# Loading two time steps at once, and only the rows that hold data, in a linear-attention and mixture-of-experts kernel

## The chip, the cores and the metric

The kernel runs on one core of a Trainium2 chip. The metric is the device time of one execution in microseconds. A comparison of this kernel with another can tell about 0.2% from no change.

The engines are called PE (matrix multiply; PEld is its weight load), DVE (vector), ACT (scalar), POOL (general purpose) and SP (which here only issues DMAs). Each engine works through its own list of instructions in order, and waits at an instruction until the semaphores it needs are set.

## The reference

The input is `r`, `k`, `v` of shape (4 batches, 8 heads, 768 tokens, 48), a decay `w` and a bonus `u` for each head and channel. The first half is a recurrence over the tokens, with a 48x48 state for each batch and head:

```python
for t in range(S):
    kt, vt, rt = (k[:, :, t], v[:, :, t], r[:, :, t])
    cur = np.einsum('bhd,bhe->bhde', u[None] * kt, vt)
    y[:, :, t] = np.einsum('bhd,bhde->bhe', rt, state + cur)
    state = w[None, :, :, None] * state + np.einsum('bhd,bhe->bhde', kt, vt)
```

The second half takes the 3072 rows of `y` (384 wide). Rows with `x @ w_skip > 0` go to one of 8 experts by the largest of `x @ w_gate`, and become `x + gate * (relu(x @ w1[e]) @ w2[e])`; the others stay as they are.

## The kernel before

**Recurrence.** The tokens are cut into chunks of 64. Two batches go together, so there are 2 x 12 = 24 steps (`NT`), step n being chunk `n % 12` of pair `n // 12`. A step needs two inputs:

- `dm`: r and k of the chunk, channels on the partitions. Two heads share a tile: rows 0 to 47 hold the channels of one, rows 64 to 111 those of the other, and rows 48 to 63 and 112 to 127 are zeros, which lie in device memory too. A step is 128 rows of 4096 bytes, one DMA of 512 KB (`load_dm`, L277), into one of four rotating buffers.
- `v`: 64 tokens of each of two batches, the tokens on the partitions. It lies in a tile `vz` whose other quadrants are zeros, written once at the start by POOL (L323), so that one matrix multiply can treat both batches. A step is two DMAs of 64 rows, 96 KB each (`load_v`, L285), into one of four lasting tiles.

**Work of a step.** `prep_r` (DVE, L418) and `prep_k` (POOL, L436) scale r and k by powers of the decay into `rd` and `kd`. On PE, `scores` (L448) multiplies them, `across` (L534) applies the state, `turn_k` (L461) transposes `kd` for the state update, `state` (L481) and `within` (L510) multiply by `v`. ACT copies the result out of PSUM (`evac`, L545), and SP writes it to device memory with two DMAs (L563; steps 4 to 7 write a third, of 192 KB).

**Order.** The order is written by hand. Iteration n of the main loop first issues on SP `load_dm(n + 5)`, `load_v(n + 4)` and in 15 of the iterations a 256 KB piece of an expert's weights (`raw`, L110). Then come `scores(n + 1)`, `across(n + 1)`, on POOL the splitting of an earlier weight piece into a high and a low part, `turn_k(n + 2)`, `prep_k(n + 3)`, `prep_r(n + 3)`, `state(n + 1)`, `within(n + 1)` and `evac(n + 1)` with its output DMAs. So `dm` of step n + 5 is issued in iteration n, scaled in iteration n + 2, and its `kd` first read by PE in iteration n + 3; `v` of step n + 4 is issued in iteration n and read by `state(n + 4)` in iteration n + 3.

A DMA on SP takes one of eight completion semaphores in turn, so each DMA waits until the one eight places before it has landed.

**Experts.** After step 23 the routed rows are gathered and the eight experts follow, with weights loaded and split ahead. Their first scratch tiles take the places of the `dm` buffers (`scratch`, L848) and of `vz`.

Of the kernel before, what the change touches and what calls it, by code (L numbers as in the profile page):

```python
# [9 lines left out]
F32 = mybir.dt.float32  # L10
# [10 lines left out]
B, H, S, D = 4, 8, 768, 48  # L21
N, DM, E, F = B * S, H * D, 8, 1024
P = 128
C = 64
# [4 lines left out]
NHP = H // 2  # L29
NT = NPAIR * NSTEP  # L30
# [8 lines left out]
DR = P  # L39
ADV = NB * NHP  # L40
BIG = 4 * N
NVK = 4
GB = 4
BH = 2
NDM = 4
# [16 lines left out]
def tile_wkv_moe(  # L62
# [11 lines left out]
    nc = tc.nc  # L74
# [168 lines left out]
        mix(y, q)  # L243


    lctx = ExitStack()
    ld = lctx.enter_context(tc.tile_pool(name="ld", bufs=NDM, side="right"))
    vctx = ExitStack()
    vp = vctx.enter_context(tc.tile_pool(name="vp", bufs=1, side="right"))
    with ExitStack() as actx:  # L250
# [17 lines left out]
        ub_sb = tab.tile([DR, NHP], F32, name="ub_sb")  # L268
        nc.scalar.dma_start(out=ub_sb, in_=ub)

        loaded = {}
        vz = [vp.tile([P, 2, 2, NHP, D], F32, name=f"vz{j}") for j in range(NVK)]

        def load_dm(n):
            pr, i = divmod(n, NSTEP)
            d = ld.tile([P, 2, NHP, 2, C], F32, tag="dm", name=f"dm{n}", bufs=NDM)
            nc.sync.dma_start(out=d, in_=dm[pr, i])  # L277
            loaded[n] = [d[:DR], None]

        def load_v(n):  # L280
            pr, i = divmod(n, NSTEP)
            t = vz[n % NVK]
            for q in range(2):
                half = slice(q * C, (q + 1) * C)
                nc.sync.dma_start(out=t[half, q], in_=tok[pr, i, half])  # L285
            loaded[n][1] = t

        load_dm(0)
        load_dm(1)
        load_v(0)  # L290
        load_dm(2)
        load_v(1)
        load_dm(3)
        load_v(2)
        load_v(3)
        wgp = tab.tile([P, NCC, 2, C // 2], F32, name="wgp")
        pick = tab.tile([P, 2, NB, E + 1], F32, name="pick")

# [21 lines left out]
        eye = lower("eye", ALU.is_equal)  # L320
        for t in vz:
            for q in range(2):
                nc.gpsimd.memset(t[(1 - q) * C : (2 - q) * C, q], 0.0)  # L323

        w_d = tab.tile([DR, NSUB, 2, NHP, C], F32, name="w_d")

# [85 lines left out]
                nc.scalar.mul(rd[:, :, 1], rd[:, :, 0], uw[:, hp : hp + 1])  # L412

        def prep_r(n, parts=(0, 1)):
            d = loaded[n][0]
            if 0 in parts:
                rds[n] = wk.tile([DR, NHP, 2, 2, C], F32, tag="rd", name=f"rd{n}", bufs=4)
                nc.vector.tensor_tensor(  # L418
                    rds[n][:, :, :, 0],
                    d[:, 0],  # L420
                    w_d[:, n % NSUB, 0][:, :, None].to_broadcast([DR, NHP, 2, C]),
                    ALU.mult,
                )
            if 1 in parts:
                rd = rds[n]
                nc.vector.tensor_tensor(
                    rd[:, :BH, :, 1],
                    rd[:, :BH, :, 0],
                    (uw if n < 3 else uw_p)[:, :BH, None, None].to_broadcast([DR, BH, 2, C]),
                    ALU.mult,  # L430
                )

        def prep_k(n, eng=None):
            d = loaded[n][0]
            kds[n] = wk.tile([DR, NHP, 2, C], F32, tag="kd", name=f"kd{n}", bufs=4)
            (eng or nc.gpsimd).tensor_tensor(  # L436
                kds[n],
                d[:, 1],
                w_d[:, n % NSUB, 1][:, :, None].to_broadcast([DR, NHP, 2, C]),
                ALU.mult,  # L440
            )
# [28 lines left out]
            nc.vector.copy_predicated(shape(am[n % 2]), eye, p[:, :, 1])  # L470

        def state(n):
            t = loaded[n][1]
            i, sub = n % NSTEP, n % NSUB
            if i == NSTEP - 1:
                return
            kt = kts.pop(n)
            s, nxt = ps_s[:, : 2 * NHP * D].rearrange("p (q f) -> p q f", q=2), sblk[(n + 1) % 2]
            for hp in range(NHP):
                for a in range(2):  # L480
                    nc.tensor.matmul(  # L481
                        s[a * C : (a + 1) * C, :, hp * D : (hp + 1) * D],
                        kt[:, hp, a, :],
                        t[:, :, a, hp, :],
                        start=i == 0 and hp == 0,
                        stop=True,
                        skip_group_check=True,
                    )
            if sub < NSUB - 1:
                nc.scalar.copy(nxt, s)  # L490
                return
            heads = lambda t: t.rearrange("p q (h e) -> p q h e", h=NHP)
            nc.vector.tensor_tensor(
                heads(nxt), heads(s), wh_sb[:, None, :, None].to_broadcast([P, NB, NHP, D]), ALU.mult
            )
            return lambda: nc.scalar.copy(s, nxt)
# [5 lines left out]
        def place_y(a, c):  # L502
            return ps_y[c * C : (c + 1) * C, a, : NHP * D].rearrange("p (q g e) -> p q g e", q=NB, g=NHP // 2)

        def within(n, behind=None):
            t = loaded[n][1]
            for g in range(NHP // 2):
                for a, c in FOUR:
                    hp = 2 * g + (a ^ c)
                    ins = nc.tensor.matmul(  # L510
                        place_y(a, c)[:, :, g, :],
                        am[n % 2][:, a, hp * C : (hp + 1) * C],
                        t[:, :, a, hp, :],
                        start=g == 0 and n % NSTEP == 0,
                        stop=True,
                        skip_group_check=True,
                    )
                    if behind is not None:
                        tc.add_manual_dep(
                            ins.ins,  # L520
                            behind.name,
                            mybir.DependencyInfo(mybir.DependencyClass.Sync, mybir.DependencyReason.DATA),
                            reason="other row tiles write these banks",
                        )
                        behind = None
# [320 lines left out]
            return banks[kind][(used[kind] - 1) % len(banks[kind])]  # L846

        def scratch(name, shape, dt, tag):  # L848
            return (ld if tag == "dm" else scr[0]).tile(
                [P] + shape, dt, tag=tag, name=name, bufs=NDM if tag == "dm" else 3  # L850
            )

        scr = []
# [14 lines left out]
        def piece(j, split=False):  # L868
            e, j = divmod(j, NPC)
            if split:  # L870
                split_piece(e, j, nc.gpsimd)
            else:
                load_piece(e, j)
# [15 lines left out]
        mask_scores(0)  # L889
        load_dm(4)  # L890
        state(0)
        turn_k(1)
        warm(1)
        within(0)
        evac(0)
        load_v(4)
        nc.sync.dma_start(out=wgp, in_=wgq)
        prep_r(2)
        bonus(2, BH)
        prep_k(2)  # L900
        grow(3)
        for n in range(NT - 1):
            if n + 5 < NT:
                load_dm(n + 5)
            if n + 4 < NT and n:
                load_v(n + 4)
            if n in LOADS:
                piece(LOADS.index(n))
            scores(n + 1)
# [37 lines left out]
        done = NPC  # L947
        piece(len(LOADS))
        vctx.close()
        scr.append(lctx.enter_context(tc.tile_pool(name="scr", bufs=3, side="right", reuse_waits="tile")))  # L950
        first = begin(0, "dm")

# [378 lines left out]
```

## Time and profile before

| what | value |
|---|---|
| median of 3 runs | 266.89 us (266.56 to 266.95) |
| profiled execution, its own time | 264.4 us |
| span in that execution, first to last instruction | 262.6 us |
| PE busy | 247.9 us (94%) |
| POOL, DVE, ACT busy | 131.7, 181.0, 140.5 us |
| moved by DMA | 53.92 MB, 205 GB/s over the span |
| first `scores` of the loop; last | 12.06 us; 107.12 us |
| granted PE clock | 0.996 |

The profile is one execution. Busy times of different engines overlap. A share of busy time averages over a recurrence of some 110 us and an expert stage of some 150 us, so stretches have to be looked at one by one. In the rows below, "A <- B" says that A stood idle until B, and the number is that idle time. SPq rows are DMA issues: their time is what SP spends on issuing, not the transfer.

### The profile page before, as it was taken

The numbers are of one execution on the slowest core, as the hardware profiler recorded it, in microseconds if no ns is written. First come the engines' busy times: TensorE is split into PE (matmuls) and PEld (weight loads), VectorE is DVE, ScalarE is ACT, GpSimd is POOL, SyncE is SP. The second block draws the span as 40 slices with busy tenths as digits, with TensorE's granted clock in tenths as the row PEclk, the third lists the DMA queues.
The fourth block names the chain that finished last, engine by engine and source line by source line (L and its number), as shares of the span: only waits on it lengthen the run. The fifth ranks groups of instructions, "written<-read, shape, count | busy, mean of one in ns | idle before, by whom it ended". The sixth has DMA issues, their size and how long they took to land.

```text
span 262.6 us, 8820 instructions
## 1 busy us (share of the span) xinstructions
PE 247.9 (94%) x3594; PEld 228.5 (87%) x3594; DVE 181.0 (69%) x366; ACT 140.5 (53%) x314; POOL 131.7 (50%) x130
## 2 busy tenths in 40 slices
PE   7799999989999999998999999999999999999990
PEld 2698898977988989877899899999999999999980
DVE  7976667786888989674567997979277484692210
ACT  2555667757865767434658628358085381660200
POOL 8656424547555365405689818454535355345011
PEclk9999999999999999999999999999999999999998
DMA  6978779899987897767798896877648475001000
GB/s 195 268 225 253 216 223 272 264 255 269 273 256 226 257 245 243 204 189 243 222 308 261 267 325 206 261 238 244 215 143 255 141 228 199 20 1 47 1 34 21
DMA packets 31137, 53.92 MB, mean 205 GB/s; under 512 B 4603, under 2 KB 14471, under 8 KB 31088
## 3 DMA queue, kind: packets, MB, share of 16 engines
q1 hardware_dynamic: 28896, 48.09, 60.5%
q0 software_dynamic: 2048, 5.18, 6.5%
q8 instruction: 30, 0.49, 0.8%
q14 instruction: 19, 0.16, 0.2%
q10 hardware_dynamic: 144, 0.00, 0.0%
HBM read 45.46 MB, written 8.39 MB: 205 GB/s over the span
## 4 chain that ended last, share of the span: by engine, by line
PE 82%; DMA 5%; DVE 4%; ACT 2%; POOL 2%; issue 1%; SPq 0%; POOLq 0%; DVEq 0%; ACTq 0%
PE ps_y L170 11%; PE ps_p L170 10%; PE ps_p L448 7%; PE ps_y L510 6%; PE ps_s L481 6%; PE ps_p L160 5%; PE ps_r L160 5%; PE ps_l L160 5%; PE ps_y L160 5%; PE ps_l L461 4%; PE ps_y L534 3%; PE ps_t L577 3%; PE ps_l L605 2%; POOL kd L436 2%; DMA xg<-out_dram,gid 2%; DMA raw<-in_w_dram 2%
## 5 line engine op out<-in xcount | busy, mean ns | idle before, releaser
L116 POOL TENSOR_TENSOR lo<-raw,hi 128x512 fp32r<-128x512 f32 x40 | 52.8, 1324 | 39.8 <-ACT hi L115 39.6
L115 ACT CAST hi<-raw 128x512 fp32r<-128x512 f32 x96 | 54.7, 623 | 1.9 <-DMA raw<-in_w_dram 1.7
L116 DVE TENSOR_TENSOR lo<-raw,hi 128x512 fp32r<-128x512 f32 x56 | 51.1, 936 | 2.5 <-ACT hi L115 2.3
L436 POOL TENSOR_TENSOR kd<-dm,w_d 128x512 f32<-128x512 f32 x23 | 33.6, 1460 | 31.5 <-DMA dm<-in_dm_dram 14.5
L178 POOL DMA_INDIRECT out_dram<-xg,sid x16 | 17.4, 1084 | 37.6 <-DVE xg L175 29.1
L469 DVE COPY_PREDICATED am<-below,ps_p 128x512 f32<-128x512 int8 x24 | 17.7, 736 | 13.4 <-PE ps_p L448 13.2
L448 PE MATMUL ps_p<-rd,kd 64*64 64x128 f32 x768 | 26.7, 276 | 0.0
L128 POOL DMA_INDIRECT xg<-out_dram,gid x16 | 18.5, 1153 | 15.3 <-DMA raw<-in_w_dram 10.6
L164 ACT ACTIVATE hh<-ps_p 128x464 fp32r<-128x464 f32 x7 | 3.9, 559 | 37.7 <-PE ps_p L160 35.7
L418 DVE TENSOR_TENSOR rd<-dm,w_d 128x512 f32<-128x512 f32 x24 | 21.9, 912 | 3.1 <-DMA dm<-in_dm_dram 3.1
L448 PEld LDWEIGHTS ps_p<-rd,kd 64*64 64x64 f32 x768 | 20.9, 133 | 3.3 <-issue 1.2
L510 PE MATMUL ps_y<-vz,am 128*64 128x96 f32 x384 | 20.3, 248 | 0.9 <-DVE am L470 0.7
L463 ACT COPY kt<-ps_l 128x512 f32<-128x512 f32 x22 | 12.9, 585 | 14.2 <-PE ps_l L461 13.9
L412 ACT ACTIVATE rd<-rd,uw 128x128 f32<-128x128 f32 x50 | 17.2, 394 | 6.0 <-DVE rd L418 5.6
L170 PE MATMUL ps_p<-hi,hh 128*128 128x384 f32 x56 | 19.4, 347 | 0.0
L170 PE MATMUL ps_p<-hi,hl 128*128 128x384 f32 x56 | 19.0, 340 | 0.4 <-DVE hl L165 0.4
L481 PE MATMUL ps_s<-vz,kt 128*64 128x96 f32 x352 | 19.4, 253 | 0.0
L170 PE MATMUL ps_y<-hi,hh 128*104 128x384 f32 x56 | 18.9, 338 | 0.0
L510 PEld LDWEIGHTS ps_y<-vz,am 128*64 128x64 f32 x384 | 17.2, 137 | 1.9 <-DVE am L470 1.1
L170 PE MATMUL ps_y<-hi,hl 128*104 128x384 f32 x56 | 18.9, 337 | 0.0
L170 PE MATMUL ps_y<-lo,hh 128*104 128x384 f32 x56 | 18.9, 337 | 0.0
L170 PE MATMUL ps_p<-lo,hh 128*128 128x384 f32 x56 | 18.8, 336 | 0.0
(252 smaller groups left out, 653.1 us busy)
## 6 DMA issues: line engine op xcount, KB each, us to landing
raw<-in_w_dram SPq DMA_DIRECT2D x96, 256.0 KB, 4.0
dm<-in_dm_dram SPq DMA_DIRECT2D x24, 512.0 KB, 5.4
vz<-in_tok_dram SPq DMA_DIRECT2D x48, 96.0 KB, 4.8
out_dram<-xt SPq DMA_DIRECT2D x48, 96.0 KB, 4.1
out_dram<-xt SPq DMA_DIRECT2D x4, 192.0 KB, 4.3
xg<-out_dram,gid POOLq DMA_INDIRECT x16, 4.8
out_dram<-xg,sid POOLq DMA_INDIRECT x16, 3.7
wgp<-in_wgq_dram SPq DMA_DIRECT2D x1, 96.0 KB, 2.1
```

The lines of the kernel that those rows point to most:

```text
L115: nc.scalar.copy(hi, t)
L116: eng.tensor_tensor(lo, t, hi.bitcast(F32), ALU.subtract)
L128: ins = nc.gpsimd.indirect_dma_start(out=xg[:m], out_offset=None, in_=out[0:rows], in_offset=bass.IndirectOffsetOnAxis(ap=gid[:m, q : q + ...
L160: nc.tensor.matmul(ph, a[:, c, fs], b[:, c, :], start=(k == 0), stop=(k == 3 * NCC - 1))
L170: nc.tensor.matmul(py, a, b[:, f, :], start=(k == 0), stop=(k == 3 * NFC - 1))
L178: ins = nc.gpsimd.indirect_dma_start(out=out, out_offset=bass.IndirectOffsetOnAxis(ap=sid[: listed(q), q : q + 1], axis=0), in_=xs.pop(q)[ ...
L418: nc.vector.tensor_tensor(rds[n][:, :, :, 0], d[:, 0], w_d[:, n % NSUB, 0][:, :, None].to_broadcast([DR, NHP, 2, C]), ALU.mult,)
L436: (eng or nc.gpsimd).tensor_tensor(kds[n], d[:, 1], w_d[:, n % NSUB, 1][:, :, None].to_broadcast([DR, NHP, 2, C]), ALU.mult,)
L448: nc.tensor.matmul(ps_p[q * C : (q + 1) * C, a, 2 * hp * C : 2 * (hp + 1) * C], kd[h, hp, q, :], rd[h, hp, q].rearrange("p s c -> p (s c)" ...
L469: nc.vector.copy_predicated(shape(am[n % 2]), below, p[:, :, 0])
L481: nc.tensor.matmul(s[a * C : (a + 1) * C, :, hp * D : (hp + 1) * D], kt[:, hp, a, :], t[:, :, a, hp, :], start=i == 0 and hp == 0, stop=Tr ...
L510: ins = nc.tensor.matmul(place_y(a, c)[:, :, g, :], am[n % 2][:, a, hp * C : (hp + 1) * C], t[:, :, a, hp, :], start=g == 0 and n % NSTEP ...
```

## The change

`dm` and `v` are loaded for two steps at a time, in odd iterations only.

- The four rotating `dm` buffers become two lasting tiles `dmz` of two steps each. Steps 0 to 3 are still loaded one by one with all 128 rows, which puts the zero rows in place. From step 4 on a load brings two steps with two DMAs, one for each half of the partitions, and only the 48 rows that hold data: 48 rows of 2 x 4096 bytes, 384 KB each.
- The four `vz` tiles become two, each for two steps. A load brings two steps with two DMAs of 64 rows, 192 KB each.
- In an odd iteration n SP issues `dm` for steps n + 5 and n + 6 and `v` for steps n + 3 and n + 4. `load_v(4)` moves from ahead of the loop into iteration 1.
- The expert stage's first scratch tiles come from the pool `scr` under the same tags, as the `dm` pool is closed by then.

The arithmetic is the same, and PE, DVE and ACT have the same instructions in the same order; POOL has four memsets of twice the size in place of eight.

```diff
+        vz = [vp.tile([P, 2, 2, 2, NHP, D], F32, name=f"vz{j}") for j in range(NVK // 2)]
+        dmz = [ld.tile([P, 2, 2, NHP, 2, C], F32, name=f"dmz{j}") for j in range(NDM // 2)]
         def load_dm(n):
             pr, i = divmod(n, NSTEP)
-            d = ld.tile([P, 2, NHP, 2, C], F32, tag="dm", name=f"dm{n}", bufs=NDM)
-            nc.sync.dma_start(out=d, in_=dm[pr, i])
-            loaded[n] = [d[:DR], None]
+            d = dmz[n % NDM // 2]
+            if n < NDM:
+                nc.sync.dma_start(out=d[:, n % 2], in_=dm[pr, i])
+                loaded[n] = d[:, n % 2]
+                return
+            for h in range(2):
+                rows = slice(h * C, h * C + D)
+                nc.sync.dma_start(
+                    out=d[rows].rearrange("p i s h q c -> p i (s h q c)"),
+                    in_=dm[pr, i : i + 2, rows].rearrange("i p s h q c -> p i (s h q c)"),
+                )
+            for j in range(2):
+                loaded[n + j] = d[:, j]
         def load_v(n):
             pr, i = divmod(n, NSTEP)
-            t = vz[n % NVK]
+            t = vz[n % NVK // 2]
             for q in range(2):
                 half = slice(q * C, (q + 1) * C)
-                nc.sync.dma_start(out=t[half, q], in_=tok[pr, i, half])
-            loaded[n][1] = t
+                nc.sync.dma_start(out=t[half, :, q], in_=tok[pr, i : i + 2, half].rearrange("i p a h d -> p i a h d"))
+            for j in range(2):
+                steps_v[n + j] = t[:, j]
         load_dm(2)
-        load_v(1)
         load_dm(3)
         load_v(2)
-        load_v(3)
...
-        load_v(4)
...
         for n in range(NT - 1):
-            if n + 5 < NT:
+            if n % 2 and n + 5 < NT:
                 load_dm(n + 5)
-            if n + 4 < NT and n:
-                load_v(n + 4)
+            if n % 2 and n + 3 < NT:
+                load_v(n + 3)
```

The first place is SP's list before the loop and at its start. Before, the kernel loads the first four steps one at a time, `v` after `dm`:

```order
L267 DMA w_in_123<-in_wd_dram 128x16
L277 DMA dm0_131<-in_dm_dram 128x1024
L277 DMA dm1_133<-in_dm_dram 128x1024
L285 DMA vz0_127<-in_tok_dram 64x384 x2
L277 DMA dm2_137<-in_dm_dram 128x1024
L285 DMA vz1_128<-in_tok_dram 64x384 x2
L277 DMA dm3_141<-in_dm_dram 128x1024
L285 DMA vz2_129<-in_tok_dram 64x384 x2
L285 DMA vz3_130<-in_tok_dram 64x384 x2
L277 DMA dm4_245<-in_dm_dram 128x1024
L563 DMA out_0_dram<-xt0_271 64x2x192 x2
L285 DMA vz0_127<-in_tok_dram 64x384 x2
```

With the change the same stretch reads:

```order
L267 DMA w_in_123<-in_wd_dram 128x16
L280 DMA dmz0_129<-in_dm_dram 128x1024 x2
L297 DMA vz0_127<-in_tok_dram 64x2x384 x2
L280 DMA dmz1_130<-in_dm_dram 128x1024 x2
L297 DMA vz1_128<-in_tok_dram 64x2x384 x2
L285 DMA dmz0_129<-in_dm_dram 48x2x1024 x2
L574 DMA out_0_dram<-xt0_259 64x2x192 x2
```

`v` of step 1 now stands ahead of `dm` of step 2, `dm` of steps 4 and 5 come together where step 4 alone stood, and `v` of step 4 is gone from here.

The second place is SP's list in iterations 7 to 9 (`dm12` is the load of iteration 7). Before:

```order
L277 DMA dm12_863<-in_dm_dram 128x1024
L285 DMA vz3_130<-in_tok_dram 64x384 x2
L563 DMA out_0_dram<-xt8_937 64x2x192 x2
L277 DMA dm13_955<-in_dm_dram 128x1024
L285 DMA vz0_127<-in_tok_dram 64x384 x2
L110 DMA raw0_3_959<-in_w12_dram 128x512
L563 DMA out_0_dram<-xt9_1040 64x2x192 x2
L277 DMA dm14_1044<-in_dm_dram 128x1024
L285 DMA vz1_128<-in_tok_dram 64x384 x2
```

With the change, from the load of steps 12 and 13 in iteration 7:

```order
L285 DMA dmz0_129<-in_dm_dram 48x2x1024 x2
L297 DMA vz1_128<-in_tok_dram 64x2x384 x2
L574 DMA out_0_dram<-xt8_909 64x2x192 x2
L110 DMA raw0_3_927<-in_w12_dram 128x512
L574 DMA out_0_dram<-xt9_1008 64x2x192 x2
L285 DMA dmz1_130<-in_dm_dram 48x2x1024 x2
L297 DMA vz0_127<-in_tok_dram 64x2x384 x2
```

Two steps take four input DMAs where they took six. `dm` of step 13 is now issued with step 12; `v` of steps 10 and 11 is issued in iteration 7, where before step 10 was issued in iteration 6 and step 11 in iteration 7.

More of the change, by code (lines that the diff above doesn't have):

```diff
@@ L243, in single @@
         mix(y, q)
-    lctx = ExitStack()
-    ld = lctx.enter_context(tc.tile_pool(name="ld", bufs=NDM, side="right"))
+    lctx, dctx = ExitStack(), ExitStack()
+    ld = dctx.enter_context(tc.tile_pool(name="ld", bufs=1, side="right"))
     vctx = ExitStack()
@@ L269, in tile_wkv_moe @@
         nc.scalar.dma_start(out=ub_sb, in_=ub)
-        loaded = {}
-        vz = [vp.tile([P, 2, 2, NHP, D], F32, name=f"vz{j}") for j in range(NVK)]
+        loaded, steps_v = {}, {}
+        vz = [vp.tile([P, 2, 2, 2, NHP, D], F32, name=f"vz{j}") for j in range(NVK // 2)]
+        dmz = [ld.tile([P, 2, 2, NHP, 2, C], F32, name=f"dmz{j}") for j in range(NDM // 2)]
         def load_dm(n):
             pr, i = divmod(n, NSTEP)
-            d = ld.tile([P, 2, NHP, 2, C], F32, tag="dm", name=f"dm{n}", bufs=NDM)
-            nc.sync.dma_start(out=d, in_=dm[pr, i])
-            loaded[n] = [d[:DR], None]
+            d = dmz[n % NDM // 2]
[11 more added lines that the diff above has]
+                loaded[n + j] = d[:, j]
         def load_v(n):
             pr, i = divmod(n, NSTEP)
-            t = vz[n % NVK]
+            t = vz[n % NVK // 2]
             for q in range(2):
                 half = slice(q * C, (q + 1) * C)
-                nc.sync.dma_start(out=t[half, q], in_=tok[pr, i, half])
-            loaded[n][1] = t
+                nc.sync.dma_start(out=t[half, :, q], in_=tok[pr, i : i + 2, half].rearrange("i p a h d -> p i a h d"))
+            for j in range(2):
+                steps_v[n + j] = t[:, j]
         load_dm(0)
@@ L322, in tile_wkv_moe @@
             for q in range(2):
-                nc.gpsimd.memset(t[(1 - q) * C : (2 - q) * C, q], 0.0)
+                nc.gpsimd.memset(t[(1 - q) * C : (2 - q) * C, :, q], 0.0)
         w_d = tab.tile([DR, NSUB, 2, NHP, C], F32, name="w_d")
@@ L414, in prep_r @@
         def prep_r(n, parts=(0, 1)):
-            d = loaded[n][0]
+            d = loaded[n]
             if 0 in parts:
@@ L433, in prep_k @@
         def prep_k(n, eng=None):
-            d = loaded[n][0]
+            d = loaded[n]
             kds[n] = wk.tile([DR, NHP, 2, C], F32, tag="kd", name=f"kd{n}", bufs=4)
@@ L472, in state @@
         def state(n):
-            t = loaded[n][1]
+            t = steps_v[n]
             i, sub = n % NSTEP, n % NSUB
@@ L505, in within @@
         def within(n, behind=None):
-            t = loaded[n][1]
+            t = steps_v[n]
             for g in range(NHP // 2):
@@ L848, in scratch @@
         def scratch(name, shape, dt, tag):
-            return (ld if tag == "dm" else scr[0]).tile(
+            return scr[0].tile(
                 [P] + shape, dt, tag=tag, name=name, bufs=NDM if tag == "dm" else 3
@@ L949, in tile_wkv_moe @@
         vctx.close()
+        dctx.close()
         scr.append(lctx.enter_context(tc.tile_pool(name="scr", bufs=3, side="right", reuse_waits="tile")))
```

## The prediction

> **What bounds the kernel now.** I read the page first, then the waits of PE, then the timeline around each wait. PE is the engine that sets the time, so what counts is where PE stands still and why.
>
> ```profile
> span 262.6 us, 8820 instructions
> PE 247.9 (94%) x3594; PEld 228.5 (87%) x3594; DVE 181.0 (69%) x366; ACT 140.5 (53%) x314; POOL 131.7 (50%) x130
> PE ps_l L461 <- POOL kd L436: 1.6, 3, 0.9
> POOL kd L436 <- DMA dm<-in_dm_dram: 14.5, 9, 4.5
> ```
>
> All of the idle time of PE is 262.6 - 247.9 = 14.7 us, most of it at the two ends. Inside the recurrence only one row leads back to the loads that change: PE waits three times, 1.6 us in total, for `kd`, and POOL, which makes `kd`, waits 14.5 us for `dm`. Those three places:
>
> ```profile
> 53.64 0.69 DVE L418 TENSOR_TENSOR rd<-dm,w_d 128x512 f32<-128x512 f32 x1 [0.34 <-DMA dm<-in_dm_dram]
> 53.78 1.72 POOL L436 TENSOR_TENSOR kd<-dm,w_d 128x512 f32<-128x512 f32 x1 [1.23 <-PE ps_y L510]
> 55.55 0.66 PE L461 MATMUL ps_l<-ident,kd 128*128 128x128 f32 x4 [0.37 <-POOL kd L436]
> ...
> 57.90 1.73 POOL L436 TENSOR_TENSOR kd<-dm,w_d 128x512 f32<-128x512 f32 x1 [2.41 <-PE ps_y L510]
> 59.69 0.66 PE L461 MATMUL ps_l<-ident,kd 128*128 128x128 f32 x4 [0.89 <-POOL kd L436]
> ...
> 71.02 1.72 POOL L436 TENSOR_TENSOR kd<-dm,w_d 128x512 f32<-128x512 f32 x1 [1.29 <-PE ps_y L510]
> 72.80 0.66 PE L461 MATMUL ps_l<-ident,kd 128*128 128x128 f32 x4 [0.33 <-POOL kd L436]
> ```
>
> POOL's own idle time is put down to PE here, but the DVE row 0.14 us earlier, which reads the same `dm`, shows the real releaser: step 12's `dm` has just landed. These are `kd` of steps 12, 13 and 16. Why is `dm` late? SP's issues:
>
> ```profile
> 18.49 0.56 SPq L277 DMA_DIRECT2D dm<-in_dm_dram  x1
> ...
> 43.80 1.46 SPq L285 DMA_DIRECT2D vz<-in_tok_dram  x2
> ...
> 47.88 1.38 SPq L277 DMA_DIRECT2D dm<-in_dm_dram  x1
> 49.36 1.15 SPq L285 DMA_DIRECT2D vz<-in_tok_dram  x2
> 50.60 1.34 SPq L563 DMA_DIRECT2D out_dram<-xt  x2
> 52.05 0.55 SPq L277 DMA_DIRECT2D dm<-in_dm_dram  x1
> 52.69 1.15 SPq L285 DMA_DIRECT2D vz<-in_tok_dram  x2
> 53.89 1.06 SPq L110 DMA_DIRECT2D raw<-in_w_dram  x1
> ...
> 58.33 0.58 SPq L110 DMA_DIRECT2D raw<-in_w_dram  x1
> ```
>
> The chain of waits has the steps' starts on PE:
>
> ```profile
> 16.08 1.07 PE ps_p L448 x31
> ...
> 37.46 1.03 PE ps_p L448 x32
> ...
> 41.33 1.03 PE ps_p L448 x32
> ```
>
> A step without extras takes PE 41.33 - 37.46 = 3.87 us. SP's list for one step, at the shortest rows, is 0.55 (`dm`) + 1.15 (`v`) + 0.58 (`raw`) + 1.34 (output) = 3.6 us, with 0.1 us or so between rows nearly 4. So SP has no slack, and falls behind: in iteration 1 `dm` goes out 18.49 - 16.08 = 2.4 us after the step's start, in iteration 7 (`dm` of step 12) 47.88 - 41.33 = 6.5 us. This lag of 4.1 us is what makes `dm` late. The transfers themselves:
>
> ```profile
> raw<-in_w_dram SPq DMA_DIRECT2D x96, 256.0 KB, 4.0
> dm<-in_dm_dram SPq DMA_DIRECT2D x24, 512.0 KB, 5.4
> vz<-in_tok_dram SPq DMA_DIRECT2D x48, 96.0 KB, 4.8
> out_dram<-xt SPq DMA_DIRECT2D x48, 96.0 KB, 4.1
> ```
>
> And how busy the 16 DMA engines are (last two columns: share, GB/s):
>
> ```profile
> 4.00:6.00 2.00, 2.00 (x10) 0.84 (x8) 1.59 (x7) 0.00 (x0) 1.81 (x5) 1.00 1.01 385
> 6.00:7.00 1.00, 0.33 (x2) 0.00 (x0) 0.97 (x3) 0.69 (x2) 0.82 (x2) 1.00 1.05 223
> 8.00:10.00 2.00, 2.00 (x51) 1.71 (x46) 2.00 (x3) 0.75 (x2) 2.00 (x2) 1.00 1.09 254
> 30.00:36.00 6.00, 6.00 (x170) 5.44 (x162) 4.29 (x6) 3.32 (x10) 1.31 (x1) 1.00 0.63 189
> 36.00:44.00 8.00, 8.00 (x214) 7.32 (x216) 5.64 (x11) 5.80 (x15) 2.45 (x2) 1.00 0.93 277
> 52.00:60.00 8.00, 6.70 (x164) 5.72 (x164) 6.68 (x16) 4.78 (x12) 4.34 (x4) 1.00 0.94 268
> 76.00:84.00 8.00, 7.81 (x194) 6.91 (x188) 6.52 (x9) 5.87 (x15) 3.85 (x3) 1.00 0.84 257
> ```
>
> From 30 to 36 us SP is already falling behind while the engines are 0.63 busy: there issuing limits, not the transfers. From 36 us on they are at 0.84 to 0.94, so the engines are close behind SP as a limit. The first three rows matter for the change. At 4 to 6 us mostly `dm` with all 128 rows moves, 385 GB/s at full share; at 6 to 7 and 8 to 10 us the 64-row halves of `v` weigh in, and the same full share moves 223 and 254.
>
> **The change part by part.** The sum is made against the profiled span, 262.6 us (its execution took 264.4, the median of the runs is 266.89; I carry the difference over unchanged).
>
> *SP's list.* Two `v` issues fewer for each pair: 2 x 1.15 / 2 = 1.15 us of SP per pair; `dm` stays at two issues. Up to step 12's load, SP now issues `v` of steps 4 to 9 with 6 DMAs, where it issued that of steps 4 to 10 with 14: 8 x 0.575 = 4.6 us less, against a lag of 4.1 us. So the lag should be gone, or nearly, by iteration 7. A new 48-row issue over two steps may cost more than 0.55 us; the nearest row of such a two-part form is the output's, 1.34 / 2 = 0.67, which takes back 0.24 per pair for `dm` and 0.19 for `v`, 1.7 us of the 4.6 over four pairs; then 1.2 us of lag stay.
>
> *`dm` of even steps (12, 16).* It comes with its partner: 768 KB (786,432 bytes) where 512 KB (524,288) came. At 277 GB/s that is 2.84 instead of 1.89 us, and the second half is issued 0.6 us later: landing after 5.4 + 0.95 + 0.6 = 6.9 us. Issued at 41.33 + 2.4 = 43.7 it lands at 50.7, with the left-over lag at 51.9; `kd` of step 12 had to start 0.37 us before 53.78, at 53.4. So it is early by 1.5 to 2.7 us: the waits of 0.37 and 0.33 go.
>
> *`dm` of odd steps (13).* It is issued one iteration sooner, with step 12, and has a step more of time: the 0.89 us go even if SP keeps its whole lag, as 47.88 + 6.9 = 54.8 is before 57.0, when `kd` would have had to start.
>
> *Fewer bytes.* 20 steps of 128 KB are not read, 2.6 MB. Hidden for PE but for the engines' share: at 277 GB/s it is 0.95 us of transfer per pair, if 48-row halves moved at that rate. They do not have to, see the rivals.
>
> *`v` gets a shorter lead.* `v` of step 10 is issued in iteration 7, not 6, behind two `dm` issues. It is read here:
>
> ```profile
> 51.93 0.88 PE L481 MATMUL ps_s<-vz,kt 128*64 128x96 f32 x16
> ```
>
> Before, it was issued at 43.80 and had 51.93 - 43.80 - 4.8 = 3.3 us to spare. Now, with the lag gone, it goes out at 43.7 + 1.2 = 44.9 and lands between 44.9 + 4.8 = 49.7 and, if it queues behind all of the 0.95 us and more that the larger loads bring (I double it), 51.6: 0.3 to 2.2 us to spare. Behind a waiting `state` stand `within` and the next `scores` on PE, so each such wait would be on the path. I take 0.2 us in all, for the tight end.
>
> *The start.* `v` of steps 0 and 1 is 197 KB more ahead of PE's first read; at 223 GB/s that is 0.9 us.
>
> ```profile
> 2.20 1.21 SPq L285 DMA_DIRECT2D vz<-in_tok_dram  x2
> 8.84 0.88 PE L481 MATMUL ps_s<-vz,kt 128*64 128x96 f32 x16
> ```
>
> Second half issued at 2.8, landing 4.8 + 0.9 later at 8.5, read at 8.84: nothing, at most 0.5 us if landing is slower by the share of 1.05. The memsets of `vz` fill the same bytes in half the instructions. The scratch tiles of the experts are written behind PE work that comes after the last read of `vz`: nothing.
>
> *After the recurrence.* PE is full, and the weight loads are issued in the same order behind it, so time saved in the recurrence stays saved:
>
> ```profile
> 160.00:200.00 40.00, 40.00 (x296) 39.49 (x295) 30.38 (x47) 23.69 (x49) 20.91 (x18) 1.00 0.68 219
> ```
>
> The sum: -0.37 - 0.89 - 0.33 + 0.2 = -1.4 us. Span 261.2, this execution 263.0, median **265.5 us**, 0.5% faster. Bounds: no more than 1.6 and some 1 us of smaller waits behind late loads, 264.3; on the other side the half-tile rate decides.
>
> **The rivals.**
>
> *Half-tile loads (slower).* Place: the DMA engines in the recurrence. `dm` was the 128-row part of the mix; now it too comes as halves. A pair cost 1,048,576 bytes / 385 = 2.7 us of full share. As 786,432 bytes at 254 GB/s it costs 3.1, at 223 it costs 3.5: the smaller load takes 0.4 to 0.8 us longer. With the engines at 0.84 to 0.94 of two steps of at least 2 x 3.87 = 7.7 us, 0.5 to 1.2 us are free. It decides from there: above that SP's eight places stay full, the lag stays, and then `v` is late. With the old lag `v` of step 10 would go out at 49.36 and land at 54.2, 2.3 us after its use at 51.93; -0.9 (odd steps) + 2.3 = +1.4, and if the engines then pace the loop by 0.8 - 0.5 = 0.3 us for each of the 6 pairs after, +3.2: 268.3 to 270.1, say 269.2. For it: the 223 and 254 rows. Against it: where `v`'s halves stand between other transfers, a lag of the 16 engines against each other can spread them, and the mix ran 277 GB/s with `v` and outputs in it.
>
> The Trainium skill, "SBUF — State Buffer", section "Door 1: The DMA port swizzle", says that a tile on partitions 0 to 63 reaches only half of the 16 ports, about 218 GB/s; the trace agrees with its 223. By that figure a pair is 786,432 / 218 = 3.6 us, an estimate from the page, and this rival would win.
>
> *Hidden (no change).* The waits of `kd` go, but `v`'s are as large, or DVE and POOL, which share the step's other work, hold PE at the same places: 266.4 to 267.4, 266.9. For it: only 1.6 us are at stake. Against: odd steps gain an iteration whatever SP does.
>
> *The lag isn't SP's.* If the eight places in flight limit and not the issue time, 10 DMAs per pair instead of 12 still help by as much: same end as the forecast, and its chance is in there.
>
> **How the numbers follow.** Forecast 0.46 (own range 264.3 to 266.3), hidden 0.22, half-tile 0.32. A measurement tells 0.2%, 0.5 us. Faster 0.46, same 0.22, slower 0.32. The range has the forecast and the hidden case, and half of the third: 264.3 to 269.3.
>
> **What would show it.** Right: no PE wait for `kd`; `dm` issued about 2.5 us after its step's start in iteration 7; DMA share below 0.85 from 52 to 60 us. Wrong: PE's `state` (now near L492) waiting for `vz`; the 48-row loads landing after more than 8 us; a share at 0.95 with fewer GB/s than 250.

## The result, and the profile after

The changed kernel takes 287.37 us (285.12 to 290.88) where the kernel before takes 266.92 us beside it: a ratio of **1.080, with a 95% interval of 1.071 to 1.089**. The forecast was 265.5 us, and a range that ended at 269.3. (Some executions of a kernel run a few per cent longer than its others at a lower clock; the ratios, and the times of run 15, leave these out, and of the profiles of runs 14 and 18, which come from such executions, only the times of DMA packets are read.) The intervals below reach 0.3 to 1.1% to each side, so a difference of less than about 1% is not told from no change here.

Where the time went. The page of the changed kernel, its first line, PE's part and the clock, then two queues:

```profile
span 285.8 us, 8772 instructions
PE 254.9 (89%) x3594; PEld 233.8 (82%) x3594; DVE 181.2 (63%) x366; ACT 139.9 (49%) x314; POOL 128.7 (45%) x126
PEclk9989999999999959999999999999999999999997
q1 hardware_dynamic: 27872, 45.47, 61.4%
q8 instruction: 30, 0.49, 0.8%
```

The span is 23.2 us longer. PE is busy 7.0 us longer with the same 3594 matrix multiplies, and idle 30.9 instead of 14.7 us. Nearly all of it lies in the recurrence. The stretch from iteration 1 to the end of the recurrence, first of the kernel before, then of the changed one (columns as in the windows shown ahead; the last three are clock, share of the DMA engines, GB/s):

```profile
16.00:113.00 97.00, 94.05 (x2396) 83.72 (x2395) 73.81 (x169) 63.85 (x157) 49.49 (x46) 1.00 0.83 243
```

```profile
16.00:135.00 119.00, 99.48 (x2389) 88.17 (x2380) 72.81 (x167) 62.60 (x155) 47.07 (x46) 0.96 0.81 176
```

The same work on PE, 22 us more. And it is the DMA side that reads worse: fewer bytes, but 0.81 x 119 = 96 us of full engines instead of 0.83 x 97 = 81. What PE waited for (us in total, times, longest):

```profile
PE ps_y L545 <- issue: 4.9, 3, 1.8
PE ps_p L459 <- issue: 4.3, 4, 1.8
PE ps_t L588 <- issue: 3.2, 1, 3.2
PE ps_r L801 <- issue: 3.0, 1, 3.0
PE ps_s L492 <- DMA vz<-in_tok_dram: 2.5, 2, 2.3
```

No row for `kd` is left, so the waits that the change could remove are gone. In their place stand 2.5 us for `v` and 15.4 us of "issue": waits that no semaphore explains, in the middle of a group of equal instructions. The longest one on PE's timeline:

```profile
65.20 0.38 PE L588 MATMUL ps_t<-ident,xt 128*128 128x128 f32 x2
68.75 0.27 PE L588 MATMUL ps_t<-ident,xt 128*128 128x128 f32 x1 [3.17 <-issue]
```

Two of three transposes of one tile run, the third 3.2 us later. The DMA view of the same time, first from 62 to 65.5 us, then from 65.5 to 67.5 (packets, MB, share of the 16 engines):

```profile
q1 hardware_dynamic: 202, 0.64, 106.7%
```

```profile
q1 hardware_dynamic: 272, 0.39, 100.2%
q8 instruction: 1, 0.02, 4.8%
```

The queue `q8`, named "instruction", moves 30 packets of 16 KB in the whole run. None comes from 62 to 65.5 us, while SP's loads (`q1`) fill the engines; one comes after 65.5, takes 4.8% of 16 x 2.0 = 1.5 us, and PE goes on 1.5 us after it is there. In the trace all seven pauses of over 1 us that are marked "issue" in the recurrence of this kernel end 1.3 to 1.5 us after the end of such a packet, and those of runs 2, 3 and 6 below end 1.2 to 1.7 us after one. So PE had run out of instructions. The Trainium skill, "Runtime: NRT & Kernel Launch", section "Instruction fetch mechanics", says that an engine refills its instructions in blocks of 16 KiB, 256 instructions, by a DMA queue of its own; the trace agrees with the size (0.49 MB in 30). It calls the cost mostly hidden; here it was not.

Why a packet comes late is not shown. It is late here while the engines are full, but full engines alone are not enough: in run 1 below (`v` in pairs, `dm` as before) they are as full in these 6 us, and PE never pauses.

```profile
62.00:68.00 6.00, 6.00 (x160) 5.37 (x155) 4.44 (x14) 4.00 (x11) 3.69 (x3) 1.00 1.03 309
```

The rest is the clock: PE is at half its clock for 3.4 us behind the pause that ended at 18.5 us, and for 6.8 us from shortly before the end of the one that ended at 101.9 us.

```profile
19.00:23.00 4.00, 4.00 (x54) 3.62 (x46) 3.90 (x9) 1.54 (x3) 3.51 (x11) 0.57 0.97 183
101.00:108.00 7.00, 6.07 (x86) 5.80 (x89) 2.71 (x12) 2.32 (x6) 0.92 (x1) 0.53 0.18 60
```

At half the clock these 10.2 us cost at most half of their length, an estimate of 5.1 of the 7.0 us by which PE is busy longer.

### The profile page after: what moved, and what is told of

Its sections match the earlier page's. It is cut to its first block, busy times and chain, and to the rows that moved or that the text cites. A ratio compares the mean times of both kernels' runs of the same rounds, so it can differ in the third digit from the quotient of the medians.

```text
span 285.8 us, 8772 instructions
## 1 busy us (share of the span) xinstructions
PE 254.9 (89%) x3594; PEld 233.8 (82%) x3594; DVE 181.2 (63%) x366; ACT 139.9 (49%) x314; POOL 128.7 (45%) x126
## 4 chain that ended last, share of the span: by engine, by line
PE 69%; DMA 11%; issue 8%; DVE 6%; ACT 3%; SPq 1%; POOL 0%; POOLq 0%; DVEq 0%; ACTq 0%
PE ps_y L170 9%; PE ps_p L170 8%; PE ps_p L459 7%; PE ps_s L492 6%; PE ps_y L521 6%; DMA vz<-in_tok_dram 5%; PE ps_p L160 4%; PE ps_r L160 4%; PE ps_l L160 4%; PE ps_y L160 4%; PE ps_l L472 3%; PE ps_y L545 3%; DMA raw<-in_w_dram 3%; PE ps_t L588 2%; PE ps_l L616 2%
## 5 line engine op out<-in xcount | busy, mean ns | idle before, releaser
L447 POOL TENSOR_TENSOR kd<-dmz,w_d 128x512 f32<-128x512 f32 x23 | 30.7, 1344 | 20.1 <-DMA dmz<-in_dm_dram 17.3
L459 PE MATMUL ps_p<-rd,kd 64*64 64x128 f32 x768 | 28.9, 282 | 4.3 <-issue 4.3
L459 PEld LDWEIGHTS ps_p<-rd,kd 64*64 64x64 f32 x768 | 22.1, 136 | 8.5 <-issue 6.5
L128 POOL DMA_INDIRECT xg<-out_dram,gid x16 | 18.5, 1155 | 15.6 <-DMA raw<-in_w_dram 10.6
L492 PE MATMUL ps_s<-vz,kt 128*64 128x96 f32 x352 | 20.9, 263 | 3.3 <-DMA vz<-in_tok_dram 2.5
L492 PEld LDWEIGHTS ps_s<-vz,kt 128*64 128x64 f32 x352 | 16.6, 144 | 7.0 <-issue 6.9
L521 PE MATMUL ps_y<-vz,am 128*64 128x96 f32 x384 | 21.5, 255 | 0.8 <-DVE am L481 0.7
L429 DVE TENSOR_TENSOR rd<-dmz,w_d 128x512 f32<-128x512 f32 x24 | 21.0, 875 | 1.2 <-DMA dmz<-in_dm_dram 1.2
L545 PE MATMUL ps_y<-sblk,rd 64*64 64x48 f32 x704 | 15.8, 220 | 5.0 <-issue 4.9
L521 PEld LDWEIGHTS ps_y<-vz,am 128*64 128x64 f32 x384 | 18.5, 143 | 1.6 <-DVE am L481 1.1
L545 PEld LDWEIGHTS ps_y<-sblk,rd 64*64 64x64 f32 x704 | 14.8, 137 | 5.6 <-issue 5.3
```

The costliest lines, as they stand in the source:

```text
L128: ins = nc.gpsimd.indirect_dma_start(out=xg[:m], out_offset=None, in_=out[0:rows], in_offset=bass.IndirectOffsetOnAxis(ap=gid[:m, q : q + ...
L429: nc.vector.tensor_tensor(rds[n][:, :, :, 0], d[:, 0], w_d[:, n % NSUB, 0][:, :, None].to_broadcast([DR, NHP, 2, C]), ALU.mult,)
L447: (eng or nc.gpsimd).tensor_tensor(kds[n], d[:, 1], w_d[:, n % NSUB, 1][:, :, None].to_broadcast([DR, NHP, 2, C]), ALU.mult,)
L459: nc.tensor.matmul(ps_p[q * C : (q + 1) * C, a, 2 * hp * C : 2 * (hp + 1) * C], kd[h, hp, q, :], rd[h, hp, q].rearrange("p s c -> p (s c)" ...
L492: nc.tensor.matmul(s[a * C : (a + 1) * C, :, hp * D : (hp + 1) * D], kt[:, hp, a, :], t[:, :, a, hp, :], start=i == 0 and hp == 0, stop=Tr ...
L521: ins = nc.tensor.matmul(place_y(a, c)[:, :, g, :], am[n % 2][:, a, hp * C : (hp + 1) * C], t[:, :, a, hp, :], start=g == 0 and n % NSTEP ...
```

## The experiments

The runs are numbered in the order of their headings. Two theories stood against each other at first. **Halves**: 48-row loads keep the DMA engines busy longer, and all that the engines carry comes late. **Pairing**: two steps' bytes in one iteration, and `v` asked for later, do it whatever the rows. Beside the ratio, one number is followed: the engine time of SP's queue, that is, the time that its packets took, as the share of `q1` in the page times the span, from one execution of each kernel: 158.9 us before (60.5% of 262.6), 175.5 us with the change, although it moves 5% fewer bytes.

### 1. Only v in pairs

```diff
-    out=d[rows] ... two 48-row loads for two steps, odd iterations
+    nc.sync.dma_start(out=d, in_=dm[pr, i])      # as before, every iteration
```

> Only half of the change: v comes for two steps at a time (64-row halves), dm stays one 128-row load per step. Halves theory (the 48-row dm loads keep the DMA engines busy for twice the time per packet, and everything else that they carry comes late): close to before, 264 to 270 us, stalls of PE inside instruction groups below 2 us in sum, dm packets as before. Pairing theory (a burst of two steps' bytes every second iteration, with v asked for one iteration later, does it, whatever the rows): half of the loss or more is back, 275 us or above, with PE waiting for vz.

Ratio **1.000** (0.996 to 1.004), queue time 159.8 us. Half of the change is free, as the halves theory had it. It is also worth nothing: 0.2 us is left of the waits for `kd`, but PE now waits 1.3 us for `rd` and 0.7 us twice on issue.

```profile
PE ps_s L482 <- ACT rd L413: 1.3, 1, 1.3
PE ps_p L449 <- issue: 0.7, 1, 0.7
```

### 2. Only dm as 48-row halves for two steps

```diff
-    t[half, :, q] <- tok[pr, i : i + 2, half]    # v for two steps, odd iterations
+    t[half, q] <- tok[pr, i, half]               # v as before
```

> The other half of the change: dm for two steps at a time as two 48-row loads, v as before (one step at a time, its old lead). Halves theory: nearly all of the loss, 278 us or above, with PE stalls inside instruction groups and the DMA share near 1 from 36 to 100 us. Pairing theory: v has its old lead and its bytes are spread again, so 272 us or less.

Ratio 1.056 (1.045 to 1.067), queue time 176.2 us. The `dm` loads carry most of the loss, `v` in pairs with its shorter lead only a part.

### 3. The pair of dm in one load of 128 rows

```diff
-    for h in range(2):
-        rows = slice(h * C, h * C + D)
-        nc.sync.dma_start(out=d[rows] ..., in_=dm[pr, i : i + 2, rows] ...)
+    nc.sync.dma_start(out=d ..., in_=dm[pr, i : i + 2] ...)
```

> The change with one thing undone: the two steps' dm come as one load of all 128 rows (1 MB) instead of two of 48 rows (768 KB); more bytes, the same pairing and the same v. Halves theory: 264 to 270 us in spite of 2.6 MB more, stalls of PE inside instruction groups back below 2 us. Pairing theory: as slow as the change or slower, 284 us or above, since the burst is larger by a third.

Ratio 1.041 (1.034 to 1.047), queue time 163.3 us. Neither theory has this: the queue time is only 4.4 us above that of before, and half of the loss stays, as waits on issue.

```profile
PE ps_s L490 <- issue: 3.6, 2, 2.6
PE ps_p L457 <- issue: 2.5, 3, 1.1
PE ps_t L586 <- issue: 2.3, 1, 2.3
PE ps_y L543 <- issue: 1.8, 1, 1.8
PE ps_r L799 <- issue: 1.7, 1, 1.7
```

### 4. The loads alone

> The kernel before, with loads alone put at its end, when nothing else moves: four loads of 1 MB with 128 rows, then the same as 64-row halves, then as 48-row halves (768 KB); each kind behind the reads of the kind before. The output is that of before; the time isn't comparable. Halves theory: 128 rows move at about 385 GB/s; 64-row halves issued one after the other at about 220 or, where two in flight cover for each other, up to 385; 48-row halves at 3/4 of the bytes no faster than the 64-row halves in time. Pairing theory: all three move at one rate, near 385, and the 48-row loads take 3/4 of the time of the 128-row loads.

DVE reads each tile when it has landed; the distance of its rows is the time of one tile's loads. 128 rows, then 64-row halves, then 48-row halves:

```profile
272.06 1.23 DVE L1112 TENSOR_SCALAR tl<-tl 128x2048 f32<-128x2048 f32 x1 [9.65 <-DMA tl<-in_dm_dram]
274.53 1.23 DVE L1112 TENSOR_SCALAR tl<-tl 128x2048 f32<-128x2048 f32 x1 [1.24 <-DMA tl<-in_dm_dram]
...
285.28 1.23 DVE L1112 TENSOR_SCALAR tl<-tl 128x2048 f32<-128x2048 f32 x1 [3.86 <-DMA tl<-in_dm_dram]
290.16 1.23 DVE L1112 TENSOR_SCALAR tl<-tl 128x2048 f32<-128x2048 f32 x1 [3.65 <-DMA tl<-in_dm_dram]
...
304.03 1.23 DVE L1112 TENSOR_SCALAR tl<-tl 128x2048 f32<-128x2048 f32 x1 [2.88 <-DMA tl<-in_dm_dram]
308.24 1.23 DVE L1112 TENSOR_SCALAR tl<-tl 128x2048 f32<-128x2048 f32 x1 [2.99 <-DMA tl<-in_dm_dram]
```

1 MB takes 2.5 us over 128 rows (the last of the four tiles 3.1) and 4.9 us as 64-row halves (215 GB/s); 768 KB as 48-row halves take 4.1 to 4.3 us (some 190 GB/s). The halves theory is right about the price.

### 5 to 8. Burst or engine time

A third theory now: **burst**. What counts is how long the loads of one iteration hold the engines, since the instruction packets stand behind them. Estimated from the loads alone (run 4): before 2.2 us, run 1 3.1, run 3 4.3, run 2 5.1, the change 6.0.

> dm as two 48-row loads, but one step at a time, every iteration (2 x 192 KB); v as before. The transfers of two iterations take the DMA engines as long as in the study of 48-row pairs with v as before, only in two parts. By the loads alone at the end of the kernel (2.5 us for 1 MB of 128 rows, 4.9 for 1 MB as 64-row halves, 4.15 for 768 KB as 48-row halves) one iteration brings 2.07 + 0.92 = 3.0 us of loads, where the v pairs alone, which cost nothing, brought 3.1 in theirs. Burst theory (what counts is how long the loads issued in one iteration keep the engines busy, since PE's instruction fetch waits behind them): 266 to 270 us, PE stalls on issue below 2 us. Occupancy theory (48-row halves cost by their engine time in sum): 280 us or above.

> The change with one thing moved: of the 48-row halves of dm for two steps the second is issued one iteration later; the same transfers, the same v. Odd iterations bring 2.07 + 1.84 = 3.9 us of loads instead of 6.0, even ones 2.07. Burst theory: on the line of the four kernels so far (3.1 us: no loss; 4.3: 11 us; 5.1: 15; 6.0: 20) some 6 us of loss, 270 to 276 us. Occupancy theory: as slow as the change, 284 us or above. A loss for want of lead would show as PE or POOL waiting for dmz.

> dm for two steps as one load of 128 rows (1 MB), v as before. 2.5 + 0.92 = 3.4 us of loads in odd iterations. Burst theory: 267 to 273 us. Rival (one load of 1 MB is what costs, v's pairing adds nothing): 276 to 279 us, as with v in pairs.

> The change with the second half of every load, dm and v, issued from ACT's queue instead of SP's, so that the two halves of the partitions can be written at the same time. The same bytes, the same tiles, the same iterations. Port theory (a half-tile load is slow because it reaches half of what takes up the data, and two halves at once fill both): dm packets of 4096 B back near 160 ns at the median, 2.07 us less and 0.92 us less in each burst, 266 to 273 us. Rival (48- and 64-row loads are slow by themselves): as slow as the change, 284 us or above.

```diff
 5:  dm[pr, i, rows] -> d[rows]              # one step, 2 x 192 KB, every iteration; v as before
 6:  load_half(n + 4, 1) in even iterations  # second half one iteration later
 7:  one 1 MB load of 128 rows for two steps; v as before
 8:  (nc.scalar if h else nc.sync).dma_start(...)   # second half of dm and v from ACT
```

Measured: one step's halves 1.037 (1.029 to 1.045), not the 266 to 270 us expected; staggered 1.046 (1.038 to 1.054), between both; 128-row pairs with single `v` 1.006 (0.999 to 1.012), as the burst theory has it; two queues 1.074 (1.064 to 1.083), nothing gained. The staggered run leaves out the second half of steps 4 and 5, so it does less than the whole work; run 13 has it whole.

Burst holds for loads of 128 rows, where pairing `dm` costs only together with pairing `v` (runs 1, 3, 7). It does not hold for the halves. In run 5 SP's list is a second difference: it has one issue more per step, and in an iteration with a weight piece and a third output it issues without a gap, 5.5 us from one `dm` to the next where a step of PE takes 3.87:

```profile
45.94 1.66 SPq L284 DMA_DIRECT2D dmz<-in_dm_dram  x2
47.69 1.17 SPq L292 DMA_DIRECT2D vz<-in_tok_dram  x2
48.90 0.58 SPq L110 DMA_DIRECT2D raw<-in_w_dram  x1
49.59 1.77 SPq L570 DMA_DIRECT2D out_dram<-xt  x3
51.47 1.00 SPq L284 DMA_DIRECT2D dmz<-in_dm_dram  x2
```

In run 8 the two halves did not run at once: in the iteration looked at (its 48 to 53 us), ACT issued its half 4.1 us before SP came to the other, and PE waited for ACT, which now waits in line with its issues. So it does not test the port theory.

```profile
PE ps_y L521 <- ACT kt L474: 7.3, 7, 2.5
```

### 9 to 12. Loads that nobody reads, and other ways to load

> The kernel with v in pairs and dm as before (no loss), plus one load of 128 rows x 2560 bytes (320 KB) in every iteration that has a dm load, into a tile that nothing reads. By the 2.5 us for 1 MB it adds 0.78 us of the engines per iteration, so that two steps hold as much load time as with the 48-row halves (5.9 us) in the parts 3.9 and 2.0, like the staggered halves; SP issues as much as before the change. No 48-row load is in it. Engine-time theory (PE's instruction fetch waits behind loads, whatever they are): 274 to 282 us, PE stalls on issue of 6 us or more, though no instruction waits for the added bytes. Row theory (48-row loads cost because their own data come late): 266 to 270 us.

```diff
+    nc.sync.dma_start(out=idle[0], in_=dm[pr, i] ... [:, :640])    # 128 rows x 2560 bytes
```

Ratio **1.055** (1.046 to 1.063), queue time 175.7 us: full loads that nothing reads cost as much as the 48-row halves, at the same queue time. The time was met, the form was not: PE waits for `v`, which stands behind them in the queue, and 1.4 us on issue in place of the 6 expected.

```profile
PE ps_s L488 <- DMA vz<-in_tok_dram: 12.7, 4, 4.2
```

> The loads alone at the end again, but of each pair of half-tile loads the second is issued from ACT's queue, and a fourth kind, 112 of the 128 rows in one load (896 KB), is added. Output as before; the time isn't comparable. Port theory (a half-tile reaches half of what takes up the data, two different halves at once fill both): 1 MB as 64-row halves in about 2.5 us instead of 4.9, the 48-row halves in about 2.1 instead of 4.15. Rival (loads of few rows are slow by themselves): 4.9 and 4.15 as from one queue. 112 rows: 2.2 us if bytes decide, 2.5 if the fuller half of the partitions does.

The 64-row halves from two queues moved 289 GB/s from 283 to 289 us, the 48-row halves 233 from 294 to 300, against 215 and 190 from one queue. So two halves at once cover for each other in part, not to the rate of 128 rows. The tiles of 112 rows landed 2.8 to 4.0 us apart, no quicker than 1 MB over 128 rows.

> The kernel before, with the second half of each v load (from step 4 on) issued by ACT instead of SP. SP is relieved of 0.58 us per step, so its lag and the 1.6 us of PE waits for kd should go; if two halves at once also take the engines less time, no PE stall comes back. 264 to 266.5 us then. Rival (ACT now waits with its issues and brings its own work late, as with everything from two queues, where PE waited 7.3 us for ACT): 268 us or more.

> v in pairs, dm one step at a time in one load, but of rows 0 to 111 alone (from step 4 on), into lasting tiles: 64 KB fewer per step without half-tile loads. If bytes decide, 0.16 us less of the engines per step; if the fuller half of the partitions decides, nothing. Either way 265 to 269 us, no stall of the halves' kind. If a load that isn't over all 128 rows is slow by itself: 272 us or above.

```diff
 11:  (nc.scalar if q and n > 3 else nc.sync).dma_start(out=t[half, q], in_=tok[pr, i, half])
 12:  rows = slice(0, P if n < NDM else C + D); dma_start(out=d[rows], in_=dm[pr, i, rows])
```

Ratios 1.008 (0.998 to 1.018) and 1.015 (1.005 to 1.024). Neither is clear of the spread of the kernel before beside it (264.3 to 270.0 us). ACT's help for SP buys nothing that can be measured, as pairing `v` bought nothing, and a load of 112 rows is no way to save the zero rows either.

### 13 to 15. Whole and clean

> The change with the second 48-row half of each pair issued one iteration later, now for all pairs. If engine time and burst add up (12 us for the staggered halves, 11 us for the burst of 128 rows alone, 20 us for the change), 276 to 281 us, with PE stalls on issue of 8 us or more. If the burst were all, 270 us or less; if engine time were all, 284 us or more.

> dm as two 48-row loads of one step in every iteration, v in pairs, so that SP issues as many loads as before. Engine time of two steps 5.9 us in the parts 3.9 and 2.07, as in the staggered run. Engine-time theory: 275 to 281 us. If the loss of one step's halves with single v (9 us) came from SP's longer list alone: 270 us or less, since the list is as short as before.

> The idle loads again at half the size: 128 rows x 1280 bytes (160 KB) per iteration with a dm load, 0.39 us of the engines each. The engines were 0.90 busy in the kernel before (mean of the stretches from 36 to 84 us), 6.9 of 7.74 us of two steps; the full dose made it 8.5, this one makes it 7.7. Threshold theory (nothing is lost until the engines fill the two steps): 266 to 272 us. Cost per byte: half of the 13.5 us, 273 to 275 us.

Staggered and whole: 1.050 (1.047 to 1.053), queue time 176.1 us. With the pair's second half moved to the next iteration, 5 of the 8% remain at the same queue time. Half the idle loads: 271.8 and 273.4 us beside 264.6 to 268.2, some 2% longer, queue time 170.8 us. One of the two times lies in the range of the threshold theory and one in that of a cost per byte, so the run does not decide between them.

Run 14 is the surprise: one step's 48-row halves in every iteration, `v` in pairs, **1.000** (0.993 to 1.007).

```profile
q1 hardware_dynamic: 28192, 45.47, 59.6%
```

The same bytes as the change and the same half-tiles, but 59.6% of 271.3 = 161.7 us of queue time instead of 175.5. So run 5's loss came from SP's list, the case named ahead of run 14; and the halves as such cost nothing when each load is short and SP's list is no longer than before.

### 16 to 18. The length of one load

> The change with each two-step 48-row load (384 KB) cut into its two steps (192 KB), in the order lower half, upper half, lower half, upper half, all in the same odd iteration; same bytes, same v, same burst. If long loads of one half of the partitions are what costs engine time, the SP queue's time falls to about 162 us (share times span) and the loss to that of the burst alone, 274 to 279 us. If the length doesn't matter and spreading over iterations did it: 284 us or more, queue time 173 us or more. If neither burst nor length is left to cost: 270 us or less.

```diff
-    for h in range(2):
-        nc.sync.dma_start(out=d[rows] ..., in_=dm[pr, i : i + 2, rows] ...)   # 384 KB
+    for j in range(2):
+        for h in range(2):
+            nc.sync.dma_start(out=d[rows, j], in_=dm[pr, i + j, rows])        # 192 KB
```

Ratio **1.011** (1.005 to 1.016). The same bytes in the same iteration from the same queue, with two issues more for each pair: queue time 162.7 us, the clock never halved in the recurrence, and 7 of the 8% are gone. What is left is `v`, behind four issues:

```profile
q1 hardware_dynamic: 28192, 45.47, 61.1%
PE ps_s L490 <- DMA vz<-in_tok_dram: 3.9, 4, 1.8
PE ps_p L457 <- issue: 1.0, 2, 0.6
```

> Loads alone at the end of the kernel before: 1 MB with 128 rows; two steps' 768 KB as two 48-row loads of 384 KB (as the change); as four of 192 KB that alternate between the halves; as four of 192 KB, two of the lower half and then two of the upper. Output as before; the time isn't comparable. If the length of a run on one half of the partitions decides: 2.5 us, 4.15, clearly less than 4.15 (3 to 3.5), 4.15. If not: 4.15 for all three, or more where four issues of 0.5 us each limit.

Alone, 768 KB as two loads of 384 KB took 4.8 us here (4.1 in run 4), as four alternating loads of 192 KB 4.2, as four in the order lower, lower, upper, upper 4.6. The first and second kind:

```profile
287.45 1.23 DVE L1115 TENSOR_SCALAR tl<-tl 128x2048 f32<-128x2048 f32 x1 [3.60 <-DMA tl<-in_dm_dram]
292.27 1.23 DVE L1115 TENSOR_SCALAR tl<-tl 128x2048 f32<-128x2048 f32 x1 [3.59 <-DMA tl<-in_dm_dram]
...
301.19 1.23 DVE L1115 TENSOR_SCALAR tl<-tl 128x2048 f32<-128x2048 f32 x1 [2.86 <-DMA tl<-in_dm_dram]
305.45 1.23 DVE L1115 TENSOR_SCALAR tl<-tl 128x2048 f32<-128x2048 f32 x1 [3.02 <-DMA tl<-in_dm_dram]
```

Within this execution shorter loads that alternate are quicker by 0.6 us, less than expected; but the two long ones took 0.6 us less than here in run 4, so alone the gain is not clear of the difference between two executions. In the kernel the queue time falls by 12.8 us over ten pairs, 1.3 us for each. There the traces show it in the `dm` packets of 4096 bytes: the median one takes 159 ns before, 316 with the change, 252 in run 16 and 166 in run 14, and 10.2 of the 12.8 us by which run 16 is below the change are time of these packets. Why a packet of a long half-tile load takes longer beside other transfers stays open.

> As the run with dm of two steps in one load of 128 rows (1 MB) and v in pairs, with that load cut into its two steps (512 KB each), issued one behind the other in the same odd iteration. The same bytes, rows and burst. If the length of a single load is what counts, with halves and without: 266 to 270 us, PE stalls on issue below 3 us. If the burst counts: 276 to 280 us as with the one load, and then short loads help the halves for another reason (two halves that cover for each other).

Ratio 1.035 (1.027 to 1.042), queue time 158.5 us. The length of a 128-row load is not what costs in run 3. Nor is it the burst as defined above: run 16 has, estimated from the loads alone, the change's 6 us of loads in one iteration, where runs 3 and 18 have 4.3, and it lost 1.1%. Why two 512 KB loads with two steps of `v` in an iteration cost 3.5% stays open. For the halves the length of each half-tile load decides.

The runs by queue time:

| kernel | queue time, us | ratio |
|---|---|---|
| before | 158.9 | 1 |
| v pairs; 128-row pairs, single v | 159.8; 155.5 | 1.000; 1.006 |
| one step's halves, v pairs; four alternating | 161.7; 162.7 | 1.000; 1.011 |
| 128-row pairs, v pairs, one load; two loads | 163.3; 158.5 | 1.041; 1.035 |
| one step's halves, single v (SP's list) | 160.7 | 1.037 |
| half the idle loads | 170.8 | some 1.02 |
| staggered; idle loads; halves with single v | 176.1; 175.7; 176.2 | 1.050; 1.055; 1.056 |
| the change | 175.5 | 1.080 |

One cause is shown. Engine time: every whole kernel with some 175 us of it lost 5.0% or more, with half-tiles or with full loads that nobody reads, and the same half-tiles in short loads, at some 162 us, lost at most 1.1% where SP's list was no longer than before. It is not all: the change loses 8.0% where the staggered loads lose 5.0% at the same engine time, and 128-row pairs with `v` in pairs lose 3.5 to 4% with hardly more of it than before. Both point to how the loads of two steps stand together, but run 16 has them together too, so this second part is measured and not explained. None of the versions is faster than the kernel before by more than can be measured.

## Why the prediction was wrong

**The waits for `kd` go: right, and worth nothing.** They are gone in the change and all but gone in run 1. Run 1 has the forecast's shorter list of SP alone, run 7 the earlier `dm` of the odd steps, and their 1.000 and 1.006 are the "hidden" rival's: in run 1 other waits came in their place.

**SP's lag goes: wrong.** SP has fewer issues, but it has to wait for the loads that are under way. In iteration 7 PE starts at 45.76 and `dm` of steps 12 and 13 goes out at 51.94, 6.2 us later instead of 2.5:

```profile
45.76 0.87 PE L459 MATMUL ps_p<-rd,kd 64*64 64x128 f32 x21
```

```profile
41.43 1.02 SPq L285 DMA_DIRECT2D dmz<-in_dm_dram  x2
...
46.42 1.73 SPq L574 DMA_DIRECT2D out_dram<-xt  x3
48.44 0.35 SPq L110 DMA_DIRECT2D raw<-in_w_dram  x1
50.17 1.65 SPq L574 DMA_DIRECT2D out_dram<-xt  x3
51.94 1.00 SPq L285 DMA_DIRECT2D dmz<-in_dm_dram  x2
```

The loads stand behind a weight piece and the output DMAs of the iteration before. The outputs' data have been ready since ACT's copy ended at 46.4 us. Both issues wait for the two 48-row loads of iteration 5, issued from 41.43 to 42.45, which are eight places before them and land only 7 and 8 us after their issue. What SP waited for from 46 to 52 us:

```profile
SPq L574 <- DMA dmz<-in_dm_dram: 1.3, 1, 1.3
SPq L110 <- DMA dmz<-in_dm_dram: 0.3, 1, 0.3
```

This is the full eight places that the half-tile rival had named. Later, from 56 to 110 us, the outputs wait for ACT, the longest time behind PE's pause that ended at 101.9 us, so a stall of PE then delays the next loads too:

```profile
SPq L574 <- ACT hi L115: 19.7, 4, 9.6
```

**`v` has 0.3 to 2.2 us to spare: wrong in size.** The chain of waits has two `v` loads that land 7.2 and 7.9 us after SP came to them, where 4.8, or twice the pair's extra 0.95 more, was reckoned; PE waited 2.5 us where 0.2 was taken.

```profile
43.81 7.16 DMA vz<-in_tok_dram
53.73 7.89 DMA vz<-in_tok_dram
```

**Fewer bytes are hidden: wrong in sign.** 5% fewer bytes took 10% more engine time.

**The step that failed** is the price of the half-tile load. It was put at so little that the forecast took it as free and left it to the rival that was given 0.32. A pair was put at 3.1 to 3.5 us against 2.7; alone it takes 4.1 to 4.8 against 2.5, 1.6 to 2.3 us more instead of 0.4 to 0.8, and more than the 0.5 to 1.2 us that were free. The rates of 223 and 254 GB/s came from stretches in which other loads moved too. The argument against this rival, that halves among other transfers need not be slow, fits the short loads of runs 14 and 16, but not loads of 384 KB; whether the engines lag against each other, as it supposed, no run shows. The Trainium skill's 218 GB/s ("SBUF — State Buffer", "Door 1: The DMA port swizzle") agrees with the 215 measured for 64 rows alone and was the better price; even so the 48-row halves were slower, 163 to 190.

**What was left out** made the rest of the miss. The rival let late loads reach PE through `kd` and `v` alone, and ended at 270.1. But PE's own instructions come over the same engines: 15.4 us of pauses on issue, and up to 5 us for the halved clock, were in no term. The sign that was named, a share near 1 at fewer GB/s, did appear: 1.00 at 184 GB/s from 52 to 60 us, where before it was 0.94 at 268.

```profile
52.00:60.00 8.00, 6.71 (x187) 5.93 (x184) 4.72 (x12) 5.46 (x14) 3.99 (x5) 1.00 1.00 184
```

## What to carry to other kernels

Where the DMA engines are 0.9 busy, price a load by the engine time it takes, not by its bytes: a long load on half of the partitions can cost more than one that also carries the zeros, and short ones that alternate between the halves less than two long ones. A wait on "issue" in the middle of a group of equal instructions is a hint to look for late instruction packets in the DMA queues. Joining the loads of several steps can cost even where no engine time is added (3.5 to 4% in runs 3 and 18), so measure each joined load alone and together with the others.

## What was not expected of the hardware

- PE's instruction packets can come late while loads fill the engines: seven pauses of 1.3 to 3.2 us in the changed kernel, against one of 0.6 us in the kernel before.
- The clock fell to half for 3.4 us or twice that at pauses of 1.8 and 3.1 us. The Trainium skill, "TensorE: Matmul & The Clock Gate", section "Part 1: The HAM clock gate (the "warmup" mystery)", asks for an idle window of about 3.4 us; here shorter pauses were enough, though not each one did it: behind the longest, 3.2 us up to 68.8 us, the clock stayed full.
- 48 rows of a half take little less time than its 64 (4.1 to 4.8 us against 4.9 for a pair), and 112 rows in one load no less than 128 (2.8 to 4.0 us against 2.5 and more).
- Two halves from two queues at once reached 289 GB/s, from one queue 215, all rows 420 (1 MB in 2.5 us).
